# A GFNet block and an MLP on one core: the last step as eight plain products, and the stores two tiles at a time

## The chip, the cores and the metric

The kernel runs on one core of a Trainium2 chip. A core has five engines that run their own instruction lists: TensorE (PE in the profile) multiplies matrices into PSUM, VectorE (DVE), ScalarE (ACT) and GpSimd (POOL) work on elements, and SyncE (SP) issues transfers between memory and SBUF, which sixteen DMA engines carry out. The metric is the device time of one execution in microseconds (us), here the median of several.

## The reference

Cut to what is computed:

```python
h = x + irfft2(rfft2(layernorm(x)) * (w_r + 1j * w_i))     # x: 1 x 2048 x 576
hid = maximum(einsum("bsd,df->bsf", layernorm(h), w1), 0)  # w1: 576 x 4608
out = h + einsum("bsf,fd->bsd", hid, w2)                   # w2: 4608 x 576
```

## The kernel before

The first part of the program computes the spectral filter as products with constant matrices, and the second layer norm. The rest is the MLP. The running sum `xs` (tile A in the profile) holds the result in SBUF as sixteen tiles of 128 tokens x 576. The hidden units are cut into 18 groups (`g`) of 256, the tokens into four chunks (`c`) of 512. A pair (g, c) is a step; there are 72, numbered 0 to 71, and the last four, 68 to 71, are the four chunks of the last group. Every fp32 number that goes into a product of the MLP is split into a high and a low part (`split`, and `relu_split` with the relu in it: ScalarE makes the high part, then VectorE, for some GpSimd, the low part as a difference), and a product is the sum of high x high, high x low and low x high.

From step 8 on a step i is a call of `slot(i)`. It does two things in turn on TensorE. `quarter(k)`, four times, computes seven matmuls of the first layer of the *next* step (`mm1`, line 149; matmuls of 128 x 128 by 128 x 512), whose hidden values stand in PSUM in half of tiles `wps[2]` and `wps[3]` (names d_2691 and d_2692; the two steps in flight use the two halves in turn). Between the quarters stand the products of its own second layer: with the hidden values as blocks A11 to A22 (first digit: which half of the 512 tokens; second: which half of the 256 units) and w2's rows and halves of its columns as B11 to B22, the result's four quarters are A·B. `slot` uses the form with **seven** products (Winograd's variant of Strassen's): sums S1 to S4 of the A blocks and T1 to T4 of the B blocks. The T are made once for a group. The S are made in every step, by `hid_a`: ScalarE copies relu of both token halves (`p0`, `p1`), GpSimd adds and subtracts (lines 598, 602, 603, 604), and then ScalarE and VectorE split the sums.

`prod` (line 613) makes one product: six matmuls of 128 x 128 by 128 x 288. It goes to one of only two PSUM tiles, bank 0 and bank 1 of `wps` (d_2800 and d_2801). Some products are laid on top of what a bank holds. `add` (line 620) is VectorE's addition of a bank to a quarter of `xs`; some banks are added to two quarters, and a bank's next product waits for the addition that reads it.

In the last group each quarter that is complete goes out by `store` (line 627), in the order (0, 0), (1, 1), (0, 1), (1, 0) of (token half, column half). A quarter lies in two tiles `t`, `t + 1` of 64 + 64 rows, and each store moves 64 rows x 288 columns of one tile: four DMAs for a quarter, sixteen for a step, all issued by SP, one after another. In odd tiles the two halves of the rows are swapped (`rows`). A DMA waits on one of eight semaphores that it shares with the eighth before it.

In the last step (71) there is no next step, so the quarters are empty and the seven products stand alone.

Of the kernel before, what the change touches and what calls it, by code (L numbers as in the profile page):

```python
# [11 lines left out]
F32R = mybir.dt.float32r  # L12
# [4 lines left out]
S, D, DFF = 2048, 576, 4608  # L17
NK = D // 2 + 1
NT = 16
# [3 lines left out]
NG = DFF // (128 * GF)  # L23
CH = 4
NC = NT // CH
# [103 lines left out]
def kernel(ctx: ExitStack, tc: tile.TileContext, x, w_r, w_i, w1, w2, cc2, c1, fb, ib, c3, out):  # L129
    nc = tc.nc  # L130
# [3 lines left out]
    def sb(shape, tag, bufs=1, dt=F32):  # L134
        n[0] += 1
        return pool.tile(shape, dt, tag=tag, name=f"{tag}_{n[0]}", bufs=bufs)
# [3 lines left out]
    def ps():  # L140
        n[0] += 1
        return psum.tile([128, 1024], F32, tag="d", name=f"d_{n[0]}", bufs=4)

    def ebuf(shape, dt=F32):
        e = sb([128, EW], "e", EB, dt)[:, :int(np.prod(shape[1:]))]
        return e.rearrange("p (a b) -> p a b", a=shape[1]) if len(shape) == 3 else e

    def mm(o, l, r, start, stop):
        nc.tensor.matmul(o, l, r, start=start, stop=stop)  # L149

    def act(o, i, **kw):
        nc.scalar.activation(o, i, AF.Copy, **kw)  # L152

    xs = sb([128, NT, D], "X")
    xv = x[0].rearrange("(h j t) d -> j h t d", j=2, t=NT)
    ov = out[0].rearrange("(h j t) d -> j h t d", j=2, t=NT)
# [150 lines left out]
    def split(h, l, v, eng=nc.vector):  # L307
        act(h, v)
        eng.tensor_sub(l, v, h)  # L309
# [3 lines left out]
    def work(k):  # L313
        for _ in range(k):
            split(*pieces.pop(0))
# [90 lines left out]
    xs = sb([128, NT, D], "A")  # L406

    def rows(t, j):
        k = 64 * (j ^ t % 2)
        return slice(k, k + 64)  # L410
# [100 lines left out]
    def mm1(i, a, part=None):  # L511
        g, c = steps[i]
        w1h, w1l = wts[g, 0]
        if a == 0 and not part:
            pend[i] = None if i >= WINO else ps()
        p = hid_p(i, a) if i >= WINO else pend[i][:, 512 * a:512 * a + 512]
        f = slice(128 * a, 128 * a + 128)
        ops = []
        for kt in range(4):
            ops += [(w1h, kt, kt), (w1h, kt, 5 + kt), (w1l, kt, kt)]  # L520
        ops += [(w1h, 4, 4), (w1l, 4, 4)]
        for n_, (w, kt, xk) in enumerate(ops):
            if part is None or n_ // 7 == part:
                mm(p, w[:, kt, f], xc[c][:, xk, :], n_ == 0, n_ == len(ops) - 1)
        if i >= WINO:
            return
        if a == GF - 1:
            p = pend.pop(i).rearrange("p (a s) -> p a s", a=GF)
            hh, hl = sb([128, GF, 512], "D", 4, F32R), sb([128, GF, 512], "D", 4, F32R)
            nc.scalar.activation(hh, p, AF.Relu)  # L530
            nc.vector.scalar_tensor_tensor(hl, p, 0.0, hh, op0=ALU.max, op1=ALU.subtract)  # L531
            hid[i] = (hh, hl)
# [22 lines left out]
    wps, fs = [], {}  # L555
    NAMES = ("B22", "T4", "B11", "B21", "T2", "T1", "T3")

    def wform(n):
        o = 6208 + 576 * NAMES.index(n)
        return tail[0][:, o:o + 288], tail[0][:, o + 288:o + 576]  # L560
# [11 lines left out]
    def wino_w(*names):  # L572
        for n in names:
            split(*wform(n), fs[n])
# [10 lines left out]
    def relu_split(f, p):  # L585
        h, l = f
        nc.scalar.activation(h, p, AF.Relu)  # L587
        nc.vector.scalar_tensor_tensor(l, p, 0.0, h, op0=ALU.max, op1=ALU.subtract)  # L588

    def hid_p(i, k):  # L590
        return wps[2 + k][:, 512 * (i % 2):512 * (i % 2) + 512]

    def hid_a(i, k):
        p = hid_p(i, k)
        if k == 0:
            relu_split(fs["A11"], p[:, :256])
            nc.scalar.activation(fs["p0"], p.rearrange("p (a n) -> p a n", a=2), AF.Relu)  # L597
            nc.gpsimd.tensor_sub(fs["S3"], fs["p0"][:, 0], fs["p0"][:, 1])  # L598
        else:
            relu_split(fs["A12"], p[:, :256])  # L600
            nc.scalar.activation(fs["p1"], p.rearrange("p (a n) -> p a n", a=2), AF.Relu)  # L601
            nc.gpsimd.tensor_add(fs["S1"], fs["p0"][:, 1], fs["p1"][:, 1])  # L602
            nc.gpsimd.tensor_sub(fs["S2"], fs["S1"], fs["p0"][:, 0])  # L603
            nc.gpsimd.tensor_sub(fs["S4"], fs["p1"][:, 0], fs["S2"])

    def prod(i, a, b, bank, first):
        ah, al = fs[a]
        bh, bl = wform(b)
        P = wps[bank].rearrange("p (a n) -> p a n", a=2)[:, :, :288]
        for tt in range(2):  # L610
            q = slice(128 * tt, 128 * tt + 128)
            for n_, (l, r) in enumerate(((ah, bh), (ah, bl), (al, bh))):
                nc.tensor.matmul(P[:, tt], l[:, q], r, start=first and n_ == 0, stop=n_ == 2, skip_group_check=not first)  # L613

    def add(i, bank, *to):
        c = steps[i][1]
        P = wps[bank].rearrange("p (a n) -> p a n", a=2)[:, :, :288]
        for hs, hd in to:
            xt = xs[:, CH * c + 2 * hs:CH * c + 2 * hs + 2, 288 * hd:288 * hd + 288]
            nc.vector.tensor_add(xt, xt, P)  # L620

    def store(c, hs, hd):
        if steps[-1][0] == NG - 1:
            t, d = CH * c + 2 * hs, slice(288 * hd, 288 * hd + 288)
            for j in range(2):
                for o in range(2):
                    nc.sync.dma_start(ov[j, :, t + o, d], xs[rows(o, j), t + o, d])

    def slot(i):
        g, c = steps[i]  # L630
        more, last, turn = i + 1 < len(steps), g == NG - 1, c == NC - 1 and g < NG - 1
        new, w1 = c == 0 and g > 2, g < NG - 1 and c in (1, 2)

        def quarter(k):
            if more:
                mm1(i + 1, k // 2, k % 2)
                if k % 2:
                    hid_a(i + 1, k // 2)

        quarter(0)  # L640
        if new:
            wino_w("T3", "B22")
        if w1:
            work(1)
        prod(i, "A11", "B11", 0, True)
        add(i, 0, (0, 0))
        prod(i, "A12", "B21", 1, True)
        split(*fs["S12f"], fs["S12"])
        add(i, 1, (0, 0))
        if w1:  # L650
            wino_sums(g + 1, *((1, 3) if c == 1 else (2, 4)))
        if last:
            store(c, 0, 0)
        quarter(1)
        prod(i, "S2f", "T2", 0, False)
        add(i, 0, (0, 1))
        split(*fs["S4f"], fs["S4"])
        prod(i, "S1f", "T1", 1, True)
        add(i, 1, (1, 1))
        if turn:  # L660
            wino_w("B11", "B21")
        if w1:
            work(1)
        if new:
            wino_w("T4")
        quarter(2)
        prod(i, "S3f", "T3", 0, False)
        add(i, 0, (1, 1))
        if last:
            store(c, 1, 1)  # L670
        if more:
            split(*fs["S3f"], fs["S3"])
        prod(i, "S4f", "B22", 1, False)
        add(i, 1, (0, 1))
        if turn:
            wino_w("T2", "T1")
        if w1 and c == 1:
            work(1)
        if last:
            store(c, 0, 1)  # L680
        quarter(3)
        prod(i, "A22", "T4", 0, False)
        add(i, 0, (1, 0))
        if more:
            relu_split(fs["A22"], hid_p(i + 1, 1)[:, 256:])
        if last:
            store(c, 1, 0)

    first = [(0, 0), (0, 1), (0, 2), (1, 0), (1, 1), (0, 3), (1, 2), (1, 3)]
    steps = first + [(g, c) for g in range(2, NG) for c in range(NC)]  # L690
# [38 lines left out]
    for i in range(3, len(steps)):  # L729
        if i + 5 < len(steps) and steps[i + 5] == (steps[i + 5][0], 0):  # L730
            load_weights(steps[i + 5][0])
        if i + 3 < len(steps) and steps[i + 3] == (steps[i + 3][0], 0):
            split_weights(steps[i + 3][0], 0)
        if i == WINO - 3:
            wino_sums(2, 1, 2, 3, 4)
        if i == WINO - 2:
            wino_w("B11", "B21", "T2", "T1", "T3")
        if i == WINO - 1:
            wps += [None, None, ps(), ps()]
            wino_tiles()  # L740
        if i == WINO:
            wps[:2] = ps(), ps()
        if i >= WINO:
            slot(i)
            continue
        for a in range(GF):
            mm1(i + 1, a)
            if i == WINO - 1:
                hid_a(i + 1, a)
        for tt in range(CH):  # L750
            mm2(i, tt)
        if i == WINO - 1:
            relu_split(fs["A22"], hid_p(i + 1, 1)[:, 256:])
            split(*fs["S3f"], fs["S3"])
            wino_w("B22", "T4")
# [22 lines left out]
```

## Time and profile before

| | |
|---|---|
| median of 3 runs | 1048.74 us (1048.67 to 1049.9) |
| the profiled execution | 1049.2 us |
| its span, first to last instruction | 1047.3 us |
| granted TensorE clock, mean | 0.994 |
| stores in the span | 64 of 72 KB, SP |
| additions of line 620 | 448, 747 ns each |
| first-layer matmuls, line 149 | 390 ns each |

A time in the profile is counted from the first instruction of the span. A matmul's duration in a row overlaps the next one's, so what a product costs is read from the distance of starts. The chain of waits is followed back from the last instruction; DMA issue on SP shows as SPq in the timeline, and issuing doesn't count as busy time. An idle time in brackets names the engine whose instruction ended it.

### The profile page before, as it was taken

The numbers are of one execution on the slowest core, as the hardware profiler recorded it, in microseconds if no ns is written. First come the engines' busy times: TensorE is split into PE (matmuls) and PEld (weight loads), VectorE is DVE, ScalarE is ACT, GpSimd is POOL, SyncE is SP. The second block draws the span as 40 slices with busy tenths as digits, with TensorE's granted clock in tenths as the row PEclk, the third lists the DMA queues.
The fourth block names the chain that finished last, engine by engine and source line by source line (L and its number), as shares of the span: only waits on it lengthen the run. The fifth ranks groups of instructions, "written<-read, shape, count | busy, mean of one in ns | idle before, by whom it ended". The sixth has DMA issues, their size and how long they took to land.

```text
span 1047.3 us, 17562 instructions
## 1 busy us (share of the span) xinstructions
PE 1022.8 (98%) x6688; PEld 908.0 (87%) x6688; DVE 749.8 (72%) x1409; ACT 397.7 (38%) x910; POOL 331.9 (32%) x438
## 2 busy tenths in 40 slices
PE   8999899999999999999999999999999999999995
PEld 7887568899999999999999999999999999999994
DVE  7588696524577777777777777877777777777774
ACT  4744263511234343343433343334333343433431
POOL 4300374300132433334242433333332324333321
PEclk9999999999999999999999999999999999999998
DMA  8942701101000000000001000000000110000034
GB/s 238 230 113 65 166 2 48 49 5 44 26 23 26 24 26 23 27 23 26 23 26 43 30 26 23 26 24 26 24 26 23 43 32 23 26 24 1 1 80 102
DMA packets 32611, 48.08 MB, mean 46 GB/s; under 512 B 3472, under 2 KB 23184, under 8 KB 32528
## 3 DMA queue, kind: packets, MB, share of 16 engines
q1 hardware_dynamic: 32528, 46.96, 16.7%
q8 instruction: 53, 0.87, 0.4%
q14 instruction: 30, 0.25, 0.1%
HBM read 42.23 MB, written 4.72 MB: 45 GB/s over the span
## 4 chain that ended last, share of the span: by engine, by line
PE 93%; DVE 3%; ACT 1%; POOL 1%; issue 0%; DMA 0%; SPq 0%; DVEq 0%; POOLq 0%; ACTq 0%
PE d L149 59%; PE d L613 34%; DVE X L477 1%; PE d L495 1%; DVE e L474 0%; ACT e L223 0%; DVE e L473 0%; DMA X<-in_A_x_dram 0%; POOL r L213 0%; DVE e L372 0%; POOL B L505 0%; DVE e L371 0%; DVE D L531 0%; DVE st L209 0%; DVE e L366 0%
## 5 line engine op out<-in xcount | busy, mean ns | idle before, releaser
L620 DVE TENSOR_TENSOR A<-A,d 128x576 f32<-128x576 f32 x448 | 334.8, 747 | 49.4 <-PE d L613 49.2
L613 PE MATMUL d<-X,D 128*128 128x288 f32 x2304 | 346.3, 294 | 1.4 <-DVE A L620 0.9
L613 PEld LDWEIGHTS d<-X,D 128*128 128x128 f32 x2304 | 328.9, 188 | 17.2 <-DVE A L620 1.1
L149 PE MATMUL d<-B,e 128*128 128x512 f32 x952 | 237.4, 390 | 0.0
L149 PEld LDWEIGHTS d<-B,e 128*128 128x128 f32 x952 | 171.9, 188 | 27.8 <-issue 0.2
L588 DVE SCALAR_TENSOR_TENSOR D<-d,D 128x256 fp32r<-128x256 f32 x192 | 81.6, 425 | 122.3 <-ACT D L587 122.3
L587 ACT ACTIVATE D<-d 128x256 fp32r<-128x256 f32 x192 | 73.5, 383 | 239.6 <-PE d L149 239.6
L602 POOL TENSOR_TENSOR e<-e 128x256 f32<-128x256 f32 x64 | 47.5, 742 | 355.2 <-ACT e L601 355.2
L149 PE MATMUL d<-C,e 128*128 128x512 f32 x476 | 119.0, 390 | 0.0
L149 PE MATMUL d<-X,e 128*128 128x512 f32 x476 | 118.8, 390 | 0.0
L152 ACT ACTIVATE X<-e 128x288 fp32r<-128x288 f32 (+2 forms) x177 | 70.4, 435 | 105.1 <-PE d L613 105.1
L309 DVE TENSOR_TENSOR D<-e,D 128x512 fp32r<-128x512 f32 (+1 forms) x128 | 92.6, 724 | 20.2 <-ACT D L152 20.2
L598 POOL TENSOR_TENSOR e<-e 128x256 f32<-128x256 f32 x64 | 47.5, 743 | 173.5 <-ACT e L597 173.5
L149 PEld LDWEIGHTS d<-C,e 128*128 128x128 f32 x476 | 85.9, 188 | 13.8
L149 PEld LDWEIGHTS d<-X,e 128*128 128x128 f32 x476 | 85.9, 188 | 13.7
L152 ACT ACTIVATE D<-e 128x512 fp32r<-128x512 f32 (+1 forms) x128 | 66.8, 522 | 75.6 <-POOL e L603 72.0
L309 DVE TENSOR_TENSOR X<-e,X 128x288 fp32r<-128x288 f32 (+2 forms) x177 | 83.2, 493 | 0.3 <-POOL r L212 0.3
L613 PEld LDWEIGHTS d<-X 128*128 128x128 f32 x384 | 58.0, 188 | 5.1 <-DVE A L620 0.2
L613 PE MATMUL d<-X 128*128 128x288 f32 x384 | 61.4, 295 | 0.0
L149 PE MATMUL d<-e,D 128*128 128x288 f32 x384 | 52.7, 296 | 0.0
L149 PEld LDWEIGHTS d<-e,D 128*128 128x128 f32 x384 | 51.9, 189 | 0.7 <-ACT e L152 0.2
L603 POOL TENSOR_TENSOR e<-e,e 128x256 f32<-128x256 f32 x64 | 50.5, 788 | 5.0
(80 smaller groups left out, 963.5 us busy)
## 6 DMA issues: line engine op xcount, KB each, us to landing
e<-in_B_w_dram SPq DMA_DIRECT2D x18, 576.0 KB, 3.8
e<-in_B_w_dram SPq DMA_DIRECT2D x18, 512.0 KB, 3.7
A<-in_A_x_dram SPq DMA_DIRECT2D x16, 288.0 KB, 9.4
out_dram<-A SPq DMA_DIRECT2D x64, 72.0 KB, 2.1
X<-in_A_x_dram SPq DMA_DIRECT2D x12, 288.0 KB, 7.7
e<-in_B_w_dram SPq DMA_DIRECT2D x36, 64.0 KB, 3.5
B<-in_A_w_r_dram SPq DMA_DIRECT2D x15, 144.5 KB, 7.1
B<-in_A_w_i_dram SPq DMA_DIRECT2D x15, 144.5 KB, 7.3
```

The lines of the kernel that those rows point to most:

```text
L149: nc.tensor.matmul(o, l, r, start=start, stop=stop)
L152: nc.scalar.activation(o, i, AF.Copy, **kw)
L309: eng.tensor_sub(l, v, h)
L477: nc.vector.tensor_add(y[:, 0:289], e0, e1)
L495: nc.tensor.transpose(pz[:, 128 * b:128 * b + 128], y[:, 128 * b:128 * b + 128], ident)
L587: nc.scalar.activation(h, p, AF.Relu)
L588: nc.vector.scalar_tensor_tensor(l, p, 0.0, h, op0=ALU.max, op1=ALU.subtract)
L598: nc.gpsimd.tensor_sub(fs["S3"], fs["p0"][:, 0], fs["p0"][:, 1])
L602: nc.gpsimd.tensor_add(fs["S1"], fs["p0"][:, 1], fs["p1"][:, 1])
L603: nc.gpsimd.tensor_sub(fs["S2"], fs["S1"], fs["p0"][:, 0])
L613: nc.tensor.matmul(P[:, tt], l[:, q], r, start=first and n_ == 0, stop=n_ == 2, skip_group_check=not first)
L620: nc.vector.tensor_add(xt, xt, P)
```

## The change

Three things change, and nothing before step 68 does.

1. The last step is no longer `slot(71)` but `slot_last(71)`: eight plain products instead of seven. Each quarter of the result has a PSUM tile of its own (bank 2 for (0, 0), 1 for (1, 0), 3 for (0, 1), 0 for (1, 1)), in which its two products are summed, and is added and stored once. Banks 2 and 3 are the tiles whose second halves hold the last step's hidden values.
2. Step 70 (`end`) prepares for that: it doesn't make p0, p1 and the sums for step 71, but splits A11, A21, A12 and A22 directly. A21 and A22 go to a new buffer A2, and B12, which the seven-product form uses only within sums, is split too, by ScalarE and GpSimd.
3. A store covers two tiles: one DMA of 64 x 2 x 288, two for a quarter. The second tile's rows lie 17 rows of the result further on for the first half and 15 rows back for the second. In the last step the second DMA of each quarter is issued by ScalarE.

```diff
-    def prod(i, a, b, bank, first):
+    def prod(i, a, b, bank, first, end=True, whole=True):
         ah, al = fs[a]
-        bh, bl = wform(b)
+        bh, bl = fs["B12f"] if b == "B12" else wform(b)
...
-                nc.tensor.matmul(P[:, tt], l[:, q], r, start=first and n_ == 0, stop=n_ == 2, skip_group_check=not first)
+                nc.tensor.matmul(P[:, tt], l[:, q], r, start=first and n_ == 0, stop=end and n_ == 2, skip_group_check=whole and not first)
...
-    def store(c, hs, hd):
+    def store(c, hs, hd, two=False):
         if steps[-1][0] == NG - 1:
             t, d = CH * c + 2 * hs, slice(288 * hd, 288 * hd + 288)
-            for j in range(2):
-                for o in range(2):
-                    nc.sync.dma_start(ov[j, :, t + o, d], xs[rows(o, j), t + o, d])
+            for k in range(2):
+                o = ov[k, :, t:t + 2, d]
+                o = bass.AP(tensor=o.tensor, offset=o.offset, ap=[list(o.ap[0]), [(1 + NT * (1 - 2 * k)) * D, 2], list(o.ap[-1])])
+                (nc.scalar if k and two else nc.sync).dma_start(o, xs[64 * k:64 * k + 64, t:t + 2, d])
+
+    def slot_last(i):
+
+        c = steps[i][1]
+        banks = {(0, 0): 2, (1, 0): 1, (0, 1): 3, (1, 1): 0}
+        for h in range(2):
+            for (hs, hd), bank in banks.items():
+                prod(i, f"A{hs + 1}{h + 1}", f"B{h + 1}{hd + 1}", bank, h == 0, h == 1, False)
+                if h:
+                    add(i, bank, (hs, hd))
+                    store(c, hs, hd, True)
...
         def quarter(k):
-            if more:
-                mm1(i + 1, k // 2, k % 2)
-                if k % 2:
-                    hid_a(i + 1, k // 2)
-
+            mm1(i + 1, k // 2, k % 2)
+            if k % 2 and end:
+                for hs in range(2):
+                    relu_split(fs[f"A{hs + 1}{k // 2 + 1}"], hid_p(i + 1, k // 2)[:, 256 * hs:256 * hs + 256])
+            elif k % 2:
+                hid_a(i + 1, k // 2)
+
+        if end:
+            A2, B = ebuf([128, 4, 256], F32R), ebuf([128, 2, 288], F32R)
+            fs["A21"], fs["B12f"] = (A2[:, 0], A2[:, 1]), (B[:, 0], B[:, 1])
+            split(*fs["B12f"], fs["B12"], eng=nc.gpsimd)
         quarter(0)
...
-        if more:
+        if not end:
             split(*fs["S3f"], fs["S3"])
...
+        A22 = fs["A22"]
+        if end:
+            fs["A22"] = A2[:, 2], A2[:, 3]
         quarter(3)
+        fs["A22"], A22 = A22, fs["A22"]
         prod(i, "A22", "T4", 0, False)
         add(i, 0, (1, 0))
-        if more:
+        fs["A22"] = A22
+        if not end:
             relu_split(fs["A22"], hid_p(i + 1, 1)[:, 256:])
...
-            slot(i)
+            (slot if i + 1 < len(steps) else slot_last)(i)
```

On TensorE the last step is the end of the list. In the rows, the first name is the PSUM tile that is written (d_2800 and d_2801: banks 0 and 1; d_2691 and d_2692: banks 2 and 3), then come the weights (X_2029: w2's forms; e_9258: B12) and the hidden blocks (D_2693: A11 and A12; D_2694: S4 and A22; D_2695: S1, S2; e_9257: A21 and A22). Before:

```order
L613 MATMUL d_2800<-X_2029,D_2693 128x288 x6
L613 MATMUL d_2801<-X_2029,D_2693 128x288 x6
L613 MATMUL d_2800<-X_2029,D_2695 128x288 x6
L613 MATMUL d_2801<-X_2029,D_2695 128x288 x6
L613 MATMUL d_2800<-X_2029 128x288 x6
L613 MATMUL d_2801<-X_2029,D_2694 128x288 x6
L613 MATMUL d_2800<-X_2029,D_2694 128x288 x6
```

And of the changed kernel:

```order
L613 MATMUL d_2691<-X_2029,D_2693 128x288 x6
L613 MATMUL d_2801<-X_2029,e_9257 128x288 x6
L613 MATMUL d_2692<-e_9258,D_2693 128x288 x6
L613 MATMUL d_2800<-e_9258,e_9257 128x288 x6
L613 MATMUL d_2691<-X_2029,D_2693 128x288 x6
L613 MATMUL d_2801<-X_2029,e_9257 128x288 x6
L613 MATMUL d_2692<-X_2029,D_2693 128x288 x6
L613 MATMUL d_2800<-X_2029,e_9257 128x288 x6
```

Six products that alternate between two banks and a seventh became two rounds over four banks.

On VectorE, step 70 and the last step in the changed kernel, from the low part of A11 on (line 588 is `relu_split`, line 309 `split`, line 620 `add`; D_2693 takes the low parts of A11, later A12, and e_9257 those of A21, later A22):

```order
L588 SCALAR_TENSOR_TENSOR D_2693<-d_2691,D_2693 128x256
L588 SCALAR_TENSOR_TENSOR e_9257<-d_2691,e_9257 128x256
L620 TENSOR_TENSOR A_1332<-A_1332,d_2800 128x2x288
L309 TENSOR_TENSOR D_2694<-e_2697,D_2694 128x256
L620 TENSOR_TENSOR A_1332<-A_1332,d_2801 128x2x288
L620 TENSOR_TENSOR A_1332<-A_1332,d_2800 128x2x288
L620 TENSOR_TENSOR A_1332<-A_1332,d_2801 128x2x288
L588 SCALAR_TENSOR_TENSOR D_2693<-d_2692,D_2693 128x256
L588 SCALAR_TENSOR_TENSOR e_9257<-d_2692,e_9257 128x256
L620 TENSOR_TENSOR A_1332<-A_1332,d_2800 128x2x288
```

The second row is new and stands ahead of the addition from bank 0, the ninth row stood behind the last one, and a split of S3 between the sixth row and the seventh is gone. Four additions from banks 2, 1, 3 and 0 follow; the seven-product form had nine rows there, seven additions and two splits.

On ScalarE the list of step 70 for step 71 and what follows, before (from the split of S1 and S2 on; lines 597 and 601 are the copies p0 and p1):

```order
L152 ACTIVATE D_2695<-e_2697 128x512
L587 ACTIVATE D_2693<-d_2691 128x256
L597 ACTIVATE e_2696<-d_2691 128x512
L152 ACTIVATE D_2694<-e_2697 128x256
L152 ACTIVATE X_2029<-e_2697 128x256
L587 ACTIVATE D_2693<-d_2692 128x256
L601 ACTIVATE e_2696<-d_2692 128x512
L587 ACTIVATE D_2694<-d_2692 128x256
L152 ACTIVATE D_2695<-e_2697 128x512
L152 ACTIVATE D_2694<-e_2697 128x256
```

And of the changed kernel, one row earlier on (e_8526 is w2 as loaded):

```order
L152 ACTIVATE e_9258<-e_8526 128x288
L152 ACTIVATE D_2695<-e_2697 128x512
L587 ACTIVATE D_2693<-d_2691 128x256
L587 ACTIVATE e_9257<-d_2691 128x256
L152 ACTIVATE D_2694<-e_2697 128x256
L587 ACTIVATE D_2693<-d_2692 128x256
L587 ACTIVATE e_9257<-d_2692 128x256
L628 DMA out_dram<-A_1332 64x2x288 x4
```

The copies and the last step's sums are gone, B12's split is first, and four stores are last. GpSimd loses the four sums for step 71 and gets the low part of B12. SP has 28 stores where it had 64.

More of the change, by code (lines that the diff above doesn't have):

```diff
@@ L620, in add @@
             nc.vector.tensor_add(xt, xt, P)
-    def store(c, hs, hd):
+    def store(c, hs, hd, two=False):
         if steps[-1][0] == NG - 1:
             t, d = CH * c + 2 * hs, slice(288 * hd, 288 * hd + 288)
-            for j in range(2):
-                for o in range(2):
-                    nc.sync.dma_start(ov[j, :, t + o, d], xs[rows(o, j), t + o, d])
+            for k in range(2):
[11 more added lines that the diff above has]
+                    store(c, hs, hd, True)
     def slot(i):
         g, c = steps[i]
-        more, last, turn = i + 1 < len(steps), g == NG - 1, c == NC - 1 and g < NG - 1
+        last, turn, end = g == NG - 1, c == NC - 1 and g < NG - 1, i + 2 == len(steps)
         new, w1 = c == 0 and g > 2, g < NG - 1 and c in (1, 2)
         def quarter(k):
-            if more:
-                mm1(i + 1, k // 2, k % 2)
-                if k % 2:
-                    hid_a(i + 1, k // 2)
+            mm1(i + 1, k // 2, k % 2)
[8 more added lines that the diff above has]
+            split(*fs["B12f"], fs["B12"], eng=nc.gpsimd)
         quarter(0)
```

## The prediction, made before the changed kernel ran

> **What bounds the kernel now.** I read the page's totals, then the chain of waits at its end, then TensorE (PE), VectorE (DVE) and SP's DMA queue by timeline over the last 30 us, then the DMA views of the same stretch. The change touches only the last two steps and the stores, so only that stretch can move.
>
> ```profile
> span 1047.3 us, 17562 instructions
> PE 1022.8 (98%) x6688; PEld 908.0 (87%) x6688; DVE 749.8 (72%) x1409; ACT 397.7 (38%) x910; POOL 331.9 (32%) x438
> ```
>
> Up to the last step TensorE is the bound (98% busy). The end of the chain of waits (start, length, what) reads otherwise:
>
> ```profile
> 1026.90 1.60 PE d L149 x7
> ...
> 1030.95 0.74 POOL e L603
> ...
> 1033.13 2.70 PE d L613 x16
> ...
> 1037.80 0.76 DVE A L620
> ```
>
> The last first-layer product ends at 1028.50. Then come ScalarE, GpSimd and VectorE, which build the sums S1 to S4 of the last step, and only then TensorE and the last addition, which ends at 1038.56. The span goes on to 1047.3: 8.74 us are neither TensorE nor VectorE. The timeline from 1038 on, the store line's own view, and what the DMA engines move from 1044.0 to 1047.3 (40 slices of 0.0825 us) say what they are:
>
> ```profile
> 1037.67 6.98 SPq L627 DMA_DIRECT2D out_dram<-A  x11
> 1037.80 0.76 DVE L620 TENSOR_TENSOR A<-A,d 128x576 f32<-128x576 f32 x1
> ```
> ```profile
> L627 SPq DMA_DIRECT2D out_dram<-A x64: 466/595/1800, 998.3 to 1044.1; - x64
> DMA to landing us min/median/max: 2.0/2.1/3.6
> ```
> ```profile
> GB/s 98 251 209 182 112 42 0 0 126 237 237 196 84 14 0 56 140 195 223 210 56 14 0 0 0 0 0 0 0 0 0 0 0 0 0 0 0 0 0 0
> ```
>
> SP issues stores one by one, 6.98 / 11 = 0.635 us apart, from before the last addition until 1044.1. The last store starts to move data 15 slices in, at 1045.24, which is 1.14 us after its issue began; its packets end at 1045.8; it lands at 1044.1 + 2.05 = 1046.15, 0.35 later; the remaining 1.15 us to 1047.3 are the program's end. So **the tail is SP's issue of sixteen stores**: it could end 5.5 us sooner if the last store were issued when the last addition ends.
>
> **The change: TensorE in the last step.** The rows of PE before, with one row of the chain for the undisturbed rate:
>
> ```profile
> 1022.14 1.58 PE d L613 x12
> ```
> ```profile
> 1028.33 0.96 PE L613 MATMUL d<-X,D 128*128 128x288 f32 x6
> 1030.14 1.89 PE L613 MATMUL d<-X,D 128*128 128x288 f32 x12 [0.86 <-DVE A L620]
> 1032.40 0.53 PE L613 MATMUL d<-X,D 128*128 128x288 f32 x2 [0.37 <-ACT D L152]
> 1033.13 1.72 PE L613 MATMUL d<-X,D 128*128 128x288 f32 x10 [0.20 <-DVE D L309]
> 1034.77 1.06 PE L613 MATMUL d<-X 128*128 128x288 f32 x6
> 1035.86 1.91 PE L613 MATMUL d<-X,D 128*128 128x288 f32 x12
> ```
>
> Twelve matmuls take 1.58, so a product of six takes 0.79. The last product of step 70 runs 1028.33 to 1029.12. Before, seven products (5.53) end at 1035.86 + 1.58 = 1037.44, so 1037.44 - 1029.12 - 5.53 = 2.79 us are waits: for bank 0, for S1 and S2 and their low part, for bank 0 twice more. After, eight products (6.32) go to four banks, none of which is read before its last product, and they need no sums. If nothing waits they end at 1029.12 + 6.32 = 1035.44: 2.79 less, 0.79 more, **2.00 us sooner**. Three waits could take their place, and I check them by rows of step 70:
>
> ```profile
> 1022.24 0.39 ACT L587 ACTIVATE D<-d 128x256 fp32r<-128x256 f32 x1 [1.78 <-PE d L149]
> 1022.66 0.42 DVE L588 SCALAR_TENSOR_TENSOR D<-d,D 128x256 fp32r<-128x256 f32 x1 [0.81 <-ACT D L587]
> 1023.00 0.74 DVE L620 TENSOR_TENSOR A<-A,d 128x576 f32<-128x576 f32 x1
> 1023.12 0.60 ACT L597 ACTIVATE e<-d 128x512 f32<-128x512 f32 x1 [0.49 <-DVE D L588]
> 1024.06 0.76 DVE L309 TENSOR_TENSOR D<-e,D 128x256 fp32r<-128x256 f32 x1 [0.31 <-ACT D L152]
> 1024.74 0.74 DVE L620 TENSOR_TENSOR A<-A,d 128x576 f32<-128x576 f32 x1
> 1025.95 0.95 PE L613 MATMUL d<-X,D 128*128 128x288 f32 x6
> ...
> 1028.59 0.39 ACT L587 ACTIVATE D<-d 128x256 fp32r<-128x256 f32 x1 [2.09 <-PE d L149]
> ...
> 1029.34 0.74 DVE L620 TENSOR_TENSOR A<-A,d 128x576 f32<-128x576 f32 x1
> ```
>
> - A21 is now split on ScalarE and VectorE where ScalarE copied both halves for the sums. Its high part starts at 1023.12 as the copy did, for 0.39; the low part on VectorE runs 1023.54 to 1023.96. Queued behind it in VectorE's order are the addition of (0,1) (now about 1023.88 to 1024.62), S4's low part (to 1025.30) and the addition of (1,1) from bank 1 (to 1025.96, before 1025.48). For that one the S4 product waits, which started at 1025.95: **0.07 us** later, taken between 0 and 0.2. GpSimd's sum and VectorE's S3 part, which stood here, are gone.
> - A22's split moves ahead of the last addition of step 70. By the same lengths, A12 takes 1028.59 to 1029.42 and A22 to 1030.30, so that addition ends near 1030.96 (before 1029.34 + 0.74 = 1030.08). Bank 0 is first needed by the fourth new product, at 1029.19 + 3 x 0.79 = 1031.56: hidden, with 0.6 to spare. The same holds for bank 3, which held A12 and A22 until 1030.30 and is needed at 1030.77.
> - B12's split (ScalarE, GpSimd) stands at the start of step 70, ten us before its use: nothing. Without that cover it would cost about what A21's pair takes, 1023.12 to 1023.96.
>
> The last product then ends at 1035.51. Before, the last addition began 1037.80 - 1037.44 = 0.36 after its product; with that it runs 1035.87 to 1036.63, **1.93 sooner** than 1038.56. The additions of the four quarters are a product apart (0.79): the first ends at 1034.26.
>
> **The change: the stores.** A store now moves 64 x 2 x 288, of which SP issues 24 in the first three steps of the last group, and SP and ScalarE issue four each in the last step. The nearest rows for a 64-row transfer of two pieces per row are the loads of x (columns: shortest, median, longest issue in ns), with the DMA engines from 100 to 130 us:
>
> ```profile
> L415 SPq DMA_DIRECT2D A<-in_A_x_dram x16: 596/605/649, 101.6 to 115.7; - x16
> ```
> ```profile
> DMA  0000799999999999999999999999999930000000
> ...
> q1 hardware_dynamic: 2304, 4.72, 72.9%
> ```
>
> Twice the pieces cost no more to issue (605 ns against 595), so SP needs 8 x 0.64 = 5.1 us a step, is idle when the last step's first store is ready, and keeps up with a pair per 0.79. ScalarE's issue is in no row: its ends are 0.47 and 1.8 us (the shortest and longest row of L627), and I take SP's 0.6, the nearest. ScalarE has nothing else queued behind these DMAs. The last pair is issued at 1036.65. If only issue counted, it would land at 1036.65 + 2.05 plus about 0.25 for its double size, 1038.95. What comes instead is **the DMA engines**. The window from 1040 to 1044, before:
>
> ```profile
> DMA packets 483, 0.44 MB, mean 111 GB/s; under 512 B 99, under 2 KB 483, under 8 KB 483
> ...
> q1 hardware_dynamic: 483, 0.44, 43.6%
> ```
>
> 0.436 x 16 engines x 4 us / 483 = 57.8 ns a packet. A 72 KB store is 80 packets, 64 rows and 16 small ones (99 of 483 are small); a new one is 144, as L415's 2304 / 16 show. Eight of them are 1152 packets, 1152 x 57.8 / 16 = 4.16 us, where the additions hand over their data in 3 x 0.79. So from the first packet, 1034.28 + 1.14 = 1035.42, to 1039.58, landed at 1039.93. Bounds: packets may overlap (a burst of weight loads from 907 to 913 us, below, moves 403 GB/s), which leaves 1038.95; or go as slowly as L415, 4.72 MB in some 21.5 us, 220 GB/s: 1.18 MB take 5.4 us, landed at 1041.15. I take 4.16, from the stores themselves.
>
> ```profile
> GB/s 0 0 0 55 0 61 89 109 143 191 328 355 403 362 403 369 389 376 342 130 184 164 21 7 0 0 0 0 0 0 0 0 0 0 0 0 0 0 0 0
> ```
>
> **Sum.** Landed 1039.93 + 1.15 for the program's end = span 1041.1, 6.2 less than 1047.3; of it 1.9 is the earlier last addition and 4.3 the shorter issue. The profiled execution took 1049.2, 1.9 over its span, so it would take 1043.0; it lies 0.46 over the median of 1048.74, so the median becomes **1042.5 us**. Waiting in the shared engines up to the slow bound adds 1.2, no waiting takes away 1.0, step 70's term is worth 0.1 either way.
>
> **The rivals.** (a) *The second engine brings nothing*: issues from SP and ScalarE are made one after another. Then the eighth issue starts at 1034.28 + 7 x 0.635 = 1038.73, lands at 1041.03: **1043.6**. For it: the trace has no two engines issuing at once. Against: the DMA engines stand at 43.6% now, so issue and not transfer is what a second issuer relieves. The Trainium skill ("DMA: Bandwidth & Descriptors", section "Issuing engines are not separate DMA queues") says that DMAs of all issuers run on the same 16 engines and that issuing from several saves only the sequencers' time, usually small beside the DMA. Here the trace has that time at 0.635 x 16 against 2.1 to land, so it is not small.
>
> (b) *ScalarE issues slowly*, 1.8 us each: its fourth starts at 1034.28 + 5.4 = 1039.68, landing 1041.98: **1044.5**. An issue doubled to 1.2 us by the double pieces stays inside (a).
>
> (c) *Slower*: the new store, whose destination steps back and forth between rows, is spread over few DMA engines. On n of them a store takes 144 x 57.8 / n ns; the 32 stores then queue from 998.3 + 1.1 on, 266 / n us. With eight engines they still keep up with the steps; the kernel gets slower than 1046.15 allows from n = 5 downwards, and with two it ends near **1135**. Against: L415 has the same 64 x 2 form and shows 9 tenths over all sixteen engines, where two could show 1. The Trainium skill (same page, section "Why a DMA increments its semaphore by 16 and not by 1") gives the engines as the largest number up to 16 that divides the slowest dimension of both sides, 64 here: sixteen, and the trace of L415 agrees.
>
> (d) *The change does not do what it says*: the tail is set by something behind the last landing. Then only the 1.9 of the additions comes, **1046.8**. Against: 1046.15 lies 1.15 before the end, and SP is at work without a gap until 1044.7.
>
> **How the numbers follow.** Forecast with its bounds (1041.4 to 1043.7) 0.75; (a) 0.11; (b) 0.07; (c) 0.03; (d) 0.04. A measurement of this kernel tells about 0.2%, 2.1 us, from no change. All but (c) and (d) are beyond that; (d) lies at its edge and is shared half and half. So faster 0.95, same 0.02, slower 0.03. The range 1041.0 to 1044.6 holds the forecast's bounds with (a) and (b), and leaves out (c), (d) and a little of runs that differ (1048.67 to 1049.9 before).
>
> **What would show it.** In the profile after: eight products of 0.79 without a wait for VectorE between them, ending near 1035.5; the last addition ending near 1036.6; SP and ScalarE both issuing within 0.1 us of each addition; DMA engines near 9 tenths from 1035.4 to 1039.6. A gap between additions and issues on ScalarE's queue means (b); engines below 7 tenths with issues apart mean (a); a start of the S4 product later than 1026.2 means that the split of A21 was mis-sized. I am wrong if the last store lands before 1038.9 or after 1042.

## The result, and the profile after

The changed kernel takes 1042.95 us (median of 6 runs, 1041.17 to 1043.31) against 1049.09 for the kernel before beside it: a ratio of 0.9938, 95% interval 0.9927 to 0.9949, or 6.1 us less. 1042.5 was forecast, with 1041.0 to 1044.6 as its range. The profiled execution took 1043.13, with a span of 1041.1.

The chain of waits at its end (start, length, what):

```profile
1026.99 1.59 PE d L149 x7
1028.58 7.16 PE d L613 x54
1035.74 0.02 issue
1035.77 0.76 DVE A L620
```

From the last first-layer product to the last addition there is nothing but TensorE: 54 matmuls without a gap, where the chain of before went through ScalarE, GpSimd and VectorE.

The timeline of the last step (start, length, engine, line, operation, how often; ACTq is ScalarE's issue of stores), first all engines, then SP's queue alone:

```profile
1028.42 1.75 PE L613 MATMUL d<-X,D 128*128 128x288 f32 x12
...
1033.38 3.14 DVE L620 TENSOR_TENSOR A<-A,d 128x576 f32<-128x576 f32 x4 [2.32 <-PE d L613]
...
1034.16 3.11 ACTq L628 DMA_DIRECT2D out_dram<-A  x4
...
1034.76 0.96 PE L613 MATMUL d<-X,e 128*128 128x288 f32 x6
```
```profile
1034.16 2.98 SPq L628 DMA_DIRECT2D out_dram<-A  x4
```

The four additions follow each other and end at 1036.52. SP and ScalarE issue beside them, both from 1034.16; the last two issues end 0.6 to 0.75 us after the last addition, where SP before issued for six. The store line's view gives issue times (ns: shortest, median, longest), and the DMA view of 1036.62 on the landing of the last pair:

```profile
L628 SPq DMA_DIRECT2D out_dram<-A x28: 595/601/1624, 998.4 to 1036.5; - x28
...
L628 ACTq DMA_DIRECT2D out_dram<-A x4: 685/708/725, 1034.2 to 1036.6; - x4
```
```profile
out_dram<-A SPq DMA_DIRECT2D x1, 144.0 KB, 3.5
out_dram<-A ACTq DMA_DIRECT2D x1, 144.0 KB, 3.6
```

The last store lands at 1036.6 + 3.6 = 1040.2, 0.9 before the end. What the DMA engines do from 1034 on (40 slices of 0.1775 us):

```profile
DMA  0000000079989999968899998799996200000000
GB/s 0 0 0 0 0 0 0 6 188 214 169 175 286 383 364 390 305 175 253 266 338 370 338 318 240 208 305 318 351 370 221 91 7 0 0 0 0 0 0 0
```

They are taken from 1035.3 to 1039.6 at 6 to 9 tenths: behind the last addition there is now 0.75 us of issue, and the rest is transfers and the program's end.

### The profile page after: what moved, and what is told of

Same layout as the page of the kernel before. It is cut to its first block, busy times and chain, and to the rows that moved or that the text cites. A ratio compares the mean times of both kernels' runs of the same rounds, so it can differ in the third digit from the quotient of the medians.

```text
span 1041.1 us, 17525 instructions
## 1 busy us (share of the span) xinstructions
PE 1022.2 (98%) x6694; PEld 908.8 (87%) x6694; DVE 746.2 (72%) x1404; ACT 395.3 (38%) x907; POOL 329.9 (32%) x435
## 4 chain that ended last, share of the span: by engine, by line
PE 94%; DVE 3%; ACT 1%; POOL 1%; issue 0%; DMA 0%; SPq 0%; DVEq 0%; ACTq 0%; POOLq 0%
PE d L149 59%; PE d L613 34%; DVE X L477 1%; PE d L495 1%; DVE e L474 0%; ACT e L223 0%; DVE e L473 0%; DMA X<-in_A_x_dram 0%; POOL r L213 0%; DVE e L372 0%; POOL B L505 0%; DVE e L371 0%; DVE D L531 0%; DVE st L209 0%; DVE e L366 0%
## 5 line engine op out<-in xcount | busy, mean ns | idle before, releaser
L613 PEld LDWEIGHTS d<-X,D 128*128 128x128 f32 x2286 | 326.4, 188 | 14.7
L309 DVE TENSOR_TENSOR D<-e,D 128x512 fp32r<-128x512 f32 x126 | 91.2, 724 | 19.5 <-ACT D L152 19.5
L152 ACT ACTIVATE D<-e 128x512 fp32r<-128x512 f32 x126 | 65.6, 521 | 73.7 <-POOL e L603 70.2
```

## The experiments

Executions of one kernel differ by a us or two, mostly ahead of the last steps: step 70's last product starts between 1026.58 and 1028.61 in these profiles. So the **tail** is counted from that start (1028.42 above, 1028.33 before) to the end of the span. Ratios are to the kernel before on the same chip.

| kernel | products, last step | stores, last step | ratio (95%) | last addition ends | tail |
|---|---|---|---|---|---|
| before | seven | 16, SP | 1 | 10.23 | 18.97 |
| changed | eight | 8, SP + ScalarE | 0.9938 (0.9927 to 0.9949) | 8.10 | 12.68 |
| e0_after | same | same | 0.9948 (0.9935 to 0.9962) | 8.10 | 12.63 |
| f0_after | same | same | 0.9936 (0.9924 to 0.9949) | | 12.60 |
| e1_products_only | eight | 16, SP | 0.9998 (0.9989 to 1.0007) | 8.09 | 19.32 |
| e2_sp_only | eight | 8, SP | 0.9957 (0.9945 to 0.9970) | 8.09 | 13.79 |
| e3_stores_only | seven | 8, SP + ScalarE | 0.9959 (0.9947 to 0.9971) | 10.57 | 14.99 |
| e6_pairs_sp_only | seven | 8, SP | 0.9967 (0.9955 to 0.9980) | 10.19 | 15.33 |
| e7_act_late_only | seven | 8, ScalarE in the last two quarters | 0.9957 (0.9944 to 0.9969) | 10.20 | 14.71 |
| e4_quarters_early | eight, quarter by quarter | 8, SP + ScalarE | 0.9935 (0.9923 to 0.9948) | 8.10 | 11.85 |
| f4_quarters_early | same | same | 0.9929 (0.9916 to 0.9943) | | 11.91 |
| e5_last_by_tile | same, last quarter by tile | 10, SP + ScalarE | 0.9933 (0.9919 to 0.9946) | 7.80 | 11.69 |
| f5_last_by_tile | same | same | 0.9929 (0.9917 to 0.9941) | | 11.61 |
| g1_same_half | eight | 8, SP + ScalarE, other order | 0.9941 (0.9925 to 0.9958) | 8.10 | 13.31 |

### The change again, and its products alone

> The changed kernel once more, on the chip that runs the other three, so that they can be compared with it. Both theories: span near 1041.1 us, ratio to the kernel before near 0.994.

e0_after is the changed kernel; its tail of 12.63 is the reference on that chip.

```diff
 # e1_products_only: the changed kernel with the stores of before
-            for k in range(2):
-                o = ov[k, :, t:t + 2, d]
...
+            for j in range(2):
+                for o in range(2):
+                    nc.sync.dma_start(ov[j, :, t + o, d], xs[rows(o, j), t + o, d])
```

> Eight plain products in the last step, but the old stores (four of 72 KB a quarter, all from SP). Theory: SP is still issuing the stores of step 70 when the last step's first quarter is complete (in the kernel before, the sixteen last issues run back to back from about 1034.5 to 1044.7), so an earlier end of TensorE and VectorE changes nothing: last addition near 1036.6, last issue near 1044.1, span within 0.3 of 1047.3. Rival (the two gains of the prediction add up, 1.9 for the products and 4.3 for the stores): span near 1045.4.

The last addition ends 2.1 us sooner, and the kernel takes as long as before (0.9998). The timeline of e1_products_only (SPq is SP's queue) and its store line:

```profile
1025.18 18.29 SPq L627 DMA_DIRECT2D out_dram<-A  x28
1026.58 1.75 PE L613 MATMUL d<-X,D 128*128 128x288 f32 x12
...
1031.53 3.14 DVE L620 TENSOR_TENSOR A<-A,d 128x576 f32<-128x576 f32 x4 [2.32 <-PE d L613]
```
```profile
L627 SPq DMA_DIRECT2D out_dram<-A x64: 466/594/1540, 996.5 to 1042.9; - x64
```

SP issues 28 stores in 18.29 us, 0.65 each, with no gap to speak of, though the four additions end at 1034.67. Its last issue is 16.3 us after step 70's last product, in the kernel before 1044.1 - 1028.33 = 15.8. So the theory held and the rival fell: sixteen stores in SP's queue outlast the last step whether it is long or short. Why the last issue comes 0.5 later here, and the tail with it 0.35, is open. The profiled execution has a span of 1045.9, but it starts its tail 1.75 us early; the tail and the ratio decide.

### The second engine

```diff
 # e2_sp_only: the changed kernel, all stores from SP
-                (nc.scalar if k and two else nc.sync).dma_start(o, xs[64 * k:64 * k + 64, t:t + 2, d])
+                nc.sync.dma_start(o, xs[64 * k:64 * k + 64, t:t + 2, d])
```

> The changed kernel with all stores from SP. Theory: eight issues 0.64 apart from 1034.2, the last at 1038.7, landing 2.4 later, span near 1042.3: the second engine is worth about 1.2 us. Rival (the sixteen DMA engines alone set the end, so that a second issuer brings nothing): span near 1041.1 as with two.

The tail is 13.79, 1.1 more than with two engines: as the theory had it. What the DMA engines move in e2_sp_only from 1034 on (slices of 0.21 us), and its store line:

```profile
GB/s 0 0 0 0 0 0 0 60 230 208 203 263 225 192 225 214 203 258 230 192 203 219 208 231 247 208 214 203 236 192 264 219 181 88 0 0 0 0 0 0
```
```profile
L628 SPq DMA_DIRECT2D out_dram<-A x32: 595/606/1252, 998.6 to 1039.0; - x32
```

The last issue begins at 1039.0, 2.3 after the last addition at 1036.70 (eight issues 0.64 apart), and the rate stays near 214 GB/s. That rate is the pace of the issue: one store of 144 KB every 0.64 us is 230 GB/s and no more. The stores don't wait for one another in the DMA engines, since each of the eight lands 2.4 to 2.5 us after its issue, the last as soon as the first. The DMA view of e2_sp_only from 1034 on:

```profile
out_dram<-A SPq DMA_DIRECT2D x8, 144.0 KB, 2.5
```

In the changed kernel the first pair lands after 2.6 (SP) and 2.9 (ScalarE), the last after 3.5 and 3.6: there the stores do wait for one another.

### The stores alone

```diff
 # e3_stores_only: the kernel before, with the two-tile store
+    def store(c, hs, hd, two=False):
...
-            store(c, 0, 0)
+            store(c, 0, 0, not more)
...
-            store(c, 1, 1)
+            store(c, 1, 1, not more)
...
-            store(c, 0, 1)
+            store(c, 0, 1, not more)
...
-            store(c, 1, 0)
+            store(c, 1, 0, not more)
 # e6_pairs_sp_only: as e3_stores_only, but none of the four has "not more"
 # e7_act_late_only: as e3_stores_only, but only (0, 1) and (1, 0) have it
```

> The seven products of before with the new stores, in the last step from two engines. Theory: the last addition stays at 1038.56, its pair of stores is issued at 1038.6 and the three last quarters share the DMA engines: landing near 1041.2, span near 1042.4, so that the products are worth 1.3 beside the new stores, not 2.0. Rival (the gains add up): 1047.3 less 4.3, span near 1043.0.

14.99: 4.0 less than before, but more than either theory gave (14.1 and 14.7). The last addition ends at 10.57, 0.34 later than in the kernel before, although only stores were changed. ScalarE's timeline in e3_stores_only (step 70's last product starts at 1028.11 there):

```profile
1031.50 0.63 ACT L152 ACTIVATE D<-e 128x512 fp32r<-128x512 f32 x1 [1.38 <-POOL e L603]
1033.55 0.72 ACTq L628 DMA_DIRECT2D out_dram<-A  x1
1034.38 0.42 ACT L152 ACTIVATE D<-e 128x256 fp32r<-128x256 f32 x1 [2.25 <-DVE A L620]
```

The high part of S4 (the third row) stands behind ScalarE's first store in its list, and that store waits for VectorE's addition. It starts at 1034.38, 6.27 after step 70's last product, in the kernel before 4.19 after (1032.52). e7 and e6 test that.

> As e3_stores_only, but ScalarE issues stores of the last two quarters only, where it has no work left behind them. Theory: in e3_stores_only ScalarE's first store waits for the first quarter's addition ahead of the high part of S4, which begins 2.1 us later than before, and the last addition ends 0.34 later: here both are as before (last addition 10.23 after the start of step 70's last product) and the end comes 0.3 to 0.5 sooner, 14.6. Rival (the lateness in e3_stores_only came from something else, DMA traffic for one): the last addition at 10.57 again, 15.0.

```profile
1031.59 0.63 ACT L152 ACTIVATE D<-e 128x512 fp32r<-128x512 f32 x1 [1.39 <-POOL e L603]
1032.39 0.42 ACT L152 ACTIVATE D<-e 128x256 fp32r<-128x256 f32 x1 [0.17 <-POOL e L604]
1037.59 1.48 ACTq L628 DMA_DIRECT2D out_dram<-A  x2
```

In e7_act_late_only (ScalarE's timeline) S4's high part starts 4.20 after the product again, the last addition ends at 10.20 as before, and the tail is 14.71, 0.28 less. The theory held. And 14.71 is what the rival of e3_stores_only gave (14.7): beside the new stores the products are worth 2.0 (14.71 to 12.68), not the 1.3 of that theory.

> The seven products of before with the new two-tile stores, all from SP. Theory: the last quarters are complete 1.1 and 0.8 apart and SP needs 1.28 for a pair, so its last issue starts about 1.1 after the last addition (at 10.23 from the start of step 70's last product) and lands 2.5 later: 14.9, as e3_stores_only (14.99): with the seven products the second engine brings nothing, since its in-order waits hold up the split of S4. Rival (the second engine is worth as much here as with eight products, 1.1): 16.1.

15.33: 0.4 over the theory, 0.8 under the rival. With seven products the second engine is worth 0.3 (from e6 to e3) or 0.6 (to e7), with eight 1.1: the earlier and closer the quarters are complete, the more issue time counts.

### What the last pair waits for

```diff
 # e4_quarters_early: the same products in another order
-        for h in range(2):
-            for (hs, hd), bank in banks.items():
+        for pair in (((0, 0), (1, 0)), ((0, 1),), ((1, 1),)):
+            for h in range(2):
+                for hs, hd in pair:
...
```

> The changed kernel with the eight products in another order: each quarter's two products (of the first two quarters taken together) follow each other, so the quarters are complete 1.6, 1.6 and 0.8 us earlier and the last one at the same time. Measured from the start of step 70's last product to the end of the span (18.97 us before, 12.68 and 12.63 in two profiles of the changed kernel). Theory: the last pair lands 3.2 (SP) and 3.8 us (ScalarE) after its issue because the earlier pairs still fill the DMA engines; alone a pair takes 2.5 and 2.9, so it lands 0.9 sooner: 11.75. Rival (the last pair's landing is the queue's own time, whatever runs beside it): 12.65, no change.

The tail fell to 11.85 with the last addition where it was (8.10). The DMA view of e4_quarters_early from 1036 to 1037, the last pair:

```profile
out_dram<-A SPq DMA_DIRECT2D x1, 144.0 KB, 2.5
out_dram<-A ACTq DMA_DIRECT2D x1, 144.0 KB, 2.9
```

2.5 and 2.9 to land where the changed kernel took 3.5 and 3.6 (the 3.2 and 3.8 of the expectation are medians of its last two pairs): the difference is the queue at the DMA engines, 0.7 us for ScalarE's store, which lands last. The rival fell.

```diff
 # e5_last_by_tile: e4, and the last quarter tile by tile
...
+        for o, bank in ((0, 0), (1, 2)):
+            for h in range(2):
+                prod(i, f"A2{h + 1}", f"B{h + 1}2", bank, h == 0, h == 1, False, (o,))
+            nc.vector.tensor_add(xs[:, t + o, d], xs[:, t + o, d], wps[bank][:, 512 * o:512 * o + 288])
+            for j, eng in enumerate((nc.sync, nc.scalar)):
+                eng.dma_start(ov[j, :, t + o, d], xs[rows(o, j), t + o, d])
```

> As e4_quarters_early, and the last quarter is computed, added and stored tile by tile, in two PSUM tiles. Theory: the last addition is half as long (0.40 for 0.76) and its stores are 72 KB, which land 0.4 sooner than 144 KB: 11.75 less 0.75, 11.0 from the start of step 70's last product. Rival (four issues instead of two for the quarter, SP 0.64 and ScalarE 0.7 each, hold up the last ones): 11.75 or more.

11.69, hardly less than e4: nearer to the rival. The store line of the last quarter in e5_last_by_tile:

```profile
L648 SPq DMA_DIRECT2D out_dram<-A x2: 547/552/556, 1035.5 to 1036.2; - x2
L648 ACTq DMA_DIRECT2D out_dram<-A x2: 563/684/804, 1035.6 to 1036.5; - x2
...
DMA to landing us min/median/max: 2.5/2.6/3.1
```

The last addition ends at 1036.11, 0.30 sooner from the product than in e4. But ScalarE's second issue begins only at 1036.5, as in e4, and the 72 KB stores land after 2.5 to 3.1, not sooner than e4's pairs. The changed kernel and both orders were then timed side by side on one chip.

> The changed kernel again, beside the two faster orders on one chip. From the start of step 70's last product to the end of the span: 12.65, as in its two profiles so far.

> The order of e4_quarters_early once more, to compare its time with the changed kernel's. Theory: 11.85 from the start of step 70's last product, as measured, so 0.8 us (0.0008 in the ratio) under f0_after. Rival (the gain of the one profile was chance): 12.6.

> The kernel of e5_last_by_tile once more. Theory: 11.7 as measured, hardly less than f4_quarters_early, since ScalarE's second issue for the quarter waits 0.3 behind its first and the small stores land later beside the others; 0.9 us under f0_after. Rival (that profile was unlucky, and halving the last addition and store is worth its 0.75): 11.0.

The tails are 12.60, 11.91 and 11.61, the medians 1042.22, 1041.42 and 1041.46. The profiles repeat within 0.1, so the gain of the order (0.7) is no chance of one profile; in the times the intervals of the three overlap. Both orders are faster than the kernel before beyond doubt, and ahead of the changed kernel by their tails.

### Two issuers on one half of the rows

> The changed kernel, but in the last step SP and ScalarE store the same 64 rows of SBUF at the same time (SP of one quarter, ScalarE of the next; two quarters wait for each other), not opposite halves. In the changed kernel the two together move 350 to 390 GB/s at their best; SP alone, one half after the other, some 214 (e2_sp_only). Theory: each half of the rows can be read at some 215 GB/s and no more, so the two together now stay near 215 throughout, the drain of 1.18 MB takes 5.5 us from its first packet and the end comes 14.4 us after the start of step 70's last product. Rival (two issuers simply keep the sixteen DMA engines fuller): 350 GB/s and more as before, 13.2 us.

```diff
 # g1_same_half: stores once two quarters are listed; SP stores the first, ScalarE the second
...
-                    store(c, hs, hd, True)
+                    done.append((hs, hd))
+                if len(done) == 2:
+                    for k in range(2):
+                        for (qs, qd), eng in zip(done, (nc.sync, nc.scalar)):
...
+                            eng.dma_start(o, xs[64 * k:64 * k + 64, t:t + 2, d])
+                    done.clear()
```

Inconclusive. The DMAs still waited for their own quarter alone, so SP issued from 1033.63 and ScalarE from 1034.44, and SP's second half ran beside ScalarE's first. The tail was 13.31, near the rival's number. What the DMA engines moved from 1034 on (slices of 0.18 us), in g1_same_half:

```profile
GB/s 0 0 0 0 26 192 224 211 211 256 186 173 199 371 378 256 243 192 192 275 263 243 307 256 269 231 224 231 333 307 211 90 6 0 0 0 0 0 0 0
```

There are stretches near 210 and others at 370, but which halves met in each isn't in this view. And the theory's 215 GB/s for a half of the rows has a plainer reading, which it did not weigh: in e2_sp_only SP's issue held the rate there.

## Why the prediction was right, point by point

**The total was right**: a span of 1041.1 was forecast and measured, and the time 0.45 from the median. That the span agrees to the tenth is partly luck: the spans of the six executions run from 1039.2 to 1041.3, and some terms below were off and cancelled. Not every step was right.

**The last step on TensorE: right.** The additions were to end 1.93 us sooner than 1038.56, at 1036.63; they ended at 1036.52, and from step 70's last product 2.1 sooner (8.10 for 10.23). None of the three waits came, and the last addition began 0.22 after its product (1034.76 + 0.79), where 0.36 had been taken.

**The 0.07 for step 70's S4 product: nothing.** The order of the queue was right, but S4's low part took 0.42 and not 0.76. Two rows of VectorE from the timeline after, and TensorE's S4 product:

```profile
1023.62 0.42 DVE L588 SCALAR_TENSOR_TENSOR e<-d,e 128x256 fp32r<-128x256 f32 x1 [0.45 <-ACT e L587]
...
1024.63 0.42 DVE L309 TENSOR_TENSOR D<-e,D 128x256 fp32r<-128x256 f32 x1
...
1026.04 0.95 PE L613 MATMUL d<-X,D 128*128 128x288 f32 x6
```

That product starts 2.38 before step 70's last one, as before (1025.95 and 1028.33). In the kernel before a GpSimd sum (line 598, 1023.79 to 1024.53) ran beside the 0.76; the change removed that sum, which the prediction noted, but it kept the length. That the sum matters could be seen in the kernel before: in its last step the same difference, with GpSimd's sums over by 1032.5, took 0.42:

```profile
1034.63 0.42 DVE L309 TENSOR_TENSOR D<-e,D 128x256 fp32r<-128x256 f32 x1
```

The Trainium skill ("SBUF — State Buffer", section "SBUF: two separate sides") says that a VectorE operation with two inputs in SBUF and a GpSimd operation that reads SBUF shut each other out of a shared pair of ports. The two lengths agree with that; no run here tried it by itself.

**The split of the gain, "of it 1.9 is the earlier last addition and 4.3 the shorter issue": right in one order only.** With the stores first it comes out: they take 4.0 off the tail (4.3 where ScalarE's store is kept out of the way of the split), and the products then another 2.3 (2.0). With the products first it doesn't: alone they bring nothing (0.9998), and the stores then bring the whole. The 1.9 counts only after SP's queue no longer outlasts the last step. The prediction had SP "at work without a gap until 1044.7" and should have drawn this from it: an addition that ends sooner ahead of a full queue changes nothing. Rival (d) gave the 1.9 of the additions without the gain of the stores; by e1_products_only that leaves the time near 1048.7 and not at 1046.8.

**The issue of the pairs: right for SP, low for ScalarE.** A two-tile store was to cost SP what the old one did: 601 ns against 595. ScalarE was taken at SP's 0.6 and needs 0.71; it kept up, since the quarters come 0.79 apart. Rivals (a) and (b) fell with that: the two issue side by side, and e2 shows what one alone would cost, 1.1, as (a) had priced it (1043.6 against 1042.5). Rival (c) fell with the 2.5 us in which a store lands.

**The DMA engines: right in place and size, by a constant that isn't one.** They were to be the bound from 1035.42 to 1039.58 at near 9 tenths; they were taken from 1035.3 to 1039.6. e4 gave the same stores more room, and the last pair landed 0.7 to 1.0 sooner. But the time for a packet, 57.8 ns, is no constant. The DMA view of the changed kernel from 1034 on gives packets, MB and share of the 16 engines by queue (q1 is SP's, q10 ScalarE's):

```profile
q1 hardware_dynamic: 576, 0.59, 28.8%
q10 hardware_dynamic: 576, 0.59, 25.7%
```

Over the 7.1 us of this view that is 53.7 ns a packet; in e2_sp_only the same 1152 packets take 69 ns each (59.1% over 8.4 us). Within the drain the rate swings between 169 and 390 GB/s while the engines are as busy. That 57.8, read from stores of 72 KB issued one by one, came so near was luck. Two more terms were off and cancelled: a pair with no other pair beside it lands in 2.5 and 2.9, not in 2.3, and from the last landing to the end it took 0.9, not 1.15.

## What to carry to other kernels

Where a queue of transfers is busy without a gap up to the end, time saved ahead of it is worth nothing until the queue is shorter; measure the parts of such a change alone before giving each a share of the gain, and each beside the other too. Here fewer and larger stores brought most (3.6 us of the tail, e6_pairs_sp_only), a second issuer 0.3 to 1.1, and an order in which results are complete earlier, so that the last stores find the DMA engines idle, 0.7. A store on an engine that still computes waits in that engine's list and holds up what stands behind it.

## What was not expected of the hardware

- A store of 144 KB issued by ScalarE cost 0.63 to 0.78 us of issue (once 1.21, in g1_same_half) against SP's 0.60. Beside SP's store of the same pair it landed later, 2.9 against 2.5 us (e4_quarters_early); no run has a store of ScalarE alone.
- With the engines 6 to 9 tenths busy, SP alone moved some 214 GB/s, storing the rows 0 to 63 and 64 to 127 in turn; SP and ScalarE together, one half each, some 275 over the whole drain (1.18 MB in 4.3 us) and 350 to 390 at their best. The Trainium skill ("SBUF — State Buffer", section "Can I just issue two DMAs to hit both halves?") says that two such DMAs at once are only 6% faster than one, since they run on the same engines. No run here settles that: SP's issue held it to 230 GB/s (e2_sp_only), so its 214 doesn't show what one half after the other could reach. The nearest row in which one issuer has a backlog, the prediction's loads of x by 64 rows from SP, moved 220 GB/s and took 9.4 us to land. The two issuers were 1.2 to 1.8 times as fast as that, which speaks against the 6%, but those are loads. That it is the opposite halves that make a difference was not settled either (g1_same_half).
- VectorE's 128 x 256 difference took 0.76 us beside a GpSimd sum and 0.42 without one, both in the kernel before (1024.06 and 1034.63); in the changed kernel, where the sum is gone, it took 0.42.
